# Two token halves of a Strassen feed-forward: chained gate and up products and seven down products in the second half, with operands stored by the first

## The chip, the cores and the metric

The kernel runs on one core of one Trainium2 chip. The metric is the device time of one execution in microseconds, as the median of several runs. All arithmetic is FP32 in the interface; the matrix products are made from FP32R operands that are split into a high part and a low remainder (`ah`/`al`, `wh`/`wl`, `dh`/`dl`), so that one product takes three matmuls per block of the contraction.

## The reference

```
x = A_x                                    # (1, 2048, 576)
sa, ca, ga, sb, cb, gb = split(silu(c) @ w_mod)
h = layernorm(x) * (1 + ca) + sa
x = x + ga * attention(h)                  # 32 heads of 18, 4 segments with a running memory
h = layernorm(x) * (1 + cb) + sb
x = x + gb * ((silu(h @ w_gate) * (h @ w_up)) @ w_down)     # 576 -> 4608 -> 576
```

The change is in the last line, the feed-forward. (One DMA of the attention part moves to another queue.)

## The kernel before, in words

The attention part runs first (up to about 659 us of the profiled execution) and leaves `x` in DRAM as `xD` and its normalized form as `xhD`. The feed-forward then works on the 2048 tokens in two halves (`t` = 0, 1) of 1024 tokens, and in each half on 18 pairs (`p`) of 128-wide blocks of the 4608 hidden columns. A pair is a 2x2x2 problem: two blocks of 512 tokens (`b`), two blocks of 288 inputs, two blocks of 128 hidden columns (`f`).

**Gate and up.** For each pair, gate (`z` = 0) and up (`z` = 1) are each computed with seven products in Winograd's form of Strassen's method instead of eight. Such a product (`m` = 1 to 7, in the order `MO7`) has 7 matmuls of 512 columns into one PSUM bank of tag `M`, of which there are four: three for each of two blocks of 128 inputs, and one that holds the last 32 inputs in three copies, for its high and low parts. So a pair has 14 steps, `k` = 0 to 13, of one product each. VectorE (DVE) adds the products up: each of `m` = 6 and 7 is added to running sums `T[0]`, `T[1]`, `m` = 5 is used twice, and `fin` adds a sum to a bank, then applies SiLU (gate, ScalarE) or multiplies up by gate (DVE). `SLOT` says which of the seven combined weights in the tile `O` a product reads, and `ACT_OP` which of the seven combined activations in `y`.

**Operands.** `load_o` loads four weight blocks of a (pair, z) into `O` (L1052); `sum_o` makes the other combinations on GpSimd (POOL), 4 for each z (L1056). `prep_w` makes `wh` on ScalarE (ACT) seven steps ahead, `wl` on DVE, and the low part of 32 partitions of the third block on POOL (L1061). The operations that subtract are put in the list `later` and issued one step later. `y` holds the activations of one half; those of half 1 are prepared by `prep2` during half 0 and kept in DRAM as `yD`. `load_y` (L1040) reloads `y` in the last pair of half 0: after each up product `m` of that pair has read its combination, that combination is loaded for half 1, in the order `MO7`.

**Down.** The products of a pair's (silu(gate) * up) with `w_down` are issued during the next pair, one `down` (L1141) at each step `k` = 4 to 11: 12 matmuls of 288 columns for 128 tokens into a two-bank PSUM tile of tag `dn` (two of these), which DVE then adds to the accumulator `acc`. `load_d` loads a block of `w_down` and multiplies it by `gb` on POOL; `prep_d` splits it. Per pair that is 8 x 12 = 96 matmuls, from 8 = 2 (f) x 2 (b) x 2 (halves of the 576 outputs) block products.

Every engine runs its own instructions in the order in which the program issues them, and so does the DMA queue of SyncE (SP), which issues nearly all transfers: a transfer that waits for its buffer holds back those behind it.

## Time and profile before

| | us |
|---|---|
| median of 3 runs (1939.92 to 1940.35) | 1940.22 |
| span of the profiled execution | 1946.8 |
| first feed-forward product to first product of half 1 | 659.2 to 1293.0 |
| half 1, to the end of its last product | 1293.0 to 1933.3 |
| start to start of two pairs in half 1 (18 pairs) | 35.28 |
| PE busy, of the span | 1901.2 (98%) |
| DVE / POOL / ACT busy | 1533.1 / 1020.6 / 824.8 |
| mean granted TensorE clock | 0.993 |

The profile is of one execution, and its span is the time from the first to the last instruction of the program. It is 6.6 us (0.3%) longer than the median of the timed runs. Times in views are counted from the start of the span. PE is TensorE's matmuls, PEld its weight loads. The end of a matmul is modelled, and consecutive ones overlap, so what a matmul costs is read from start to start.

### The profile page before, as it was taken

The numbers are of one execution on the slowest core, as the hardware profiler recorded it, in microseconds if no ns is written. First come the engines' busy times: TensorE is split into PE (matmuls) and PEld (weight loads), VectorE is DVE, ScalarE is ACT, GpSimd is POOL, SyncE is SP. The second block draws the span as 40 slices with busy tenths as digits, with TensorE's granted clock in tenths as the row PEclk, the third lists the DMA queues.
The fourth block names the chain that finished last, engine by engine and source line by source line (L and its number), as shares of the span: only waits on it lengthen the run. The fifth ranks groups of instructions, "written<-read, shape, count | busy, mean of one in ns | idle before, by whom it ended". The sixth has DMA issues, their size and how long they took to land.

```text
span 1946.8 us, 31901 instructions
## 1 busy us (share of the span) xinstructions
PE 1901.2 (98%) x11119; PEld 1593.1 (82%) x11119; DVE 1533.1 (79%) x3218; ACT 824.8 (42%) x1652; POOL 1020.6 (52%) x1396
## 2 busy tenths in 40 slices
...
GB/s 207 244 227 233 203 204 140 131 139 150 136 128 125 92 135 101 89 106 80 80 106 83 82 84 78 60 264 146 74 62 45 74 62 59 60 62 74 62 57 50
DMA packets 114354, 223.59 MB, mean 115 GB/s; under 512 B 22992, under 2 KB 40784, under 8 KB 112720
## 3 DMA queue, kind: packets, MB, share of 16 engines
q1 hardware_dynamic: 111936, 215.61, 34.2%
q0 software_dynamic: 576, 5.11, 0.7%
...
## 4 chain that ended last, share of the span: by engine, by line
PE 88%; DVE 4%; DMA 4%; ACT 1%; issue 1%; POOL 1%; SPq 1%; POOLq 0%; ACTq 0%; DVEq 0%
PE M L1090 39%; PE pd L1152 23%; PE pp L93 4%; PE s L576 4%; PE av L596 4%; PE s L174 4%; PE pv L93 3%; PE pw L694 2%; DMA O<-in_wgu_dram 1%; DMA mD<-mr 1%; PE pn L765 1%; PE pm L429 1%; PE px L617 1%; PE pr L346 1%; DVE y L923 1%
## 5 line engine op out<-in xcount | busy, mean ns | idle before, releaser
L1090 PE MATMUL M<-y,wh 128*128 128x512 f32 x2520 | 792.0, 393 | 5.0 <-DVE cu L1106 2.1
L1090 PEld LDWEIGHTS M<-y,wh 128*128 128x128 f32 x2520 | 473.7, 188 | 101.7 <-issue 3.9
L1067 POOL TENSOR_TENSOR wh<-O,wh 32x128 fp32r<-32x128 f32 x504 | 296.6, 593 | 423.0 <-ACT wh L1065 271.3
L1090 PE MATMUL M<-y,wl 128*128 128x512 f32 x1008 | 394.7, 392 | 0.0
L1059 POOL TENSOR_TENSOR O<-O 128x384 f32<-128x384 f32 x288 | 315.4, 1095 | 75.0 <-DMA O<-in_wgu_dram 42.9
L1152 PE MATMUL pd<-dh,ah 128*128 128x288 f32 x1152 | 340.3, 295 | 0.2 <-DVE acc L1155 0.2
L1152 PE MATMUL pd<-dl,ah 128*128 128x288 f32 x1152 | 340.3, 295 | 0.0
L1152 PE MATMUL pd<-dh,al 128*128 128x288 f32 x1152 | 340.1, 295 | 0.0
L1110 ACT CAST ah<-sg 128x512 fp32r<-128x512 f32 x144 | 89.5, 621 | 547.8 <-DVE sg L1107 422.0
L1155 DVE TENSOR_TENSOR acc<-acc,pd 128x576 f32<-128x576 f32 x288 | 216.5, 752 | 111.8 <-PE pd L1152 108.4
L1066 DVE TENSOR_TENSOR wl<-O,wh 128x256 fp32r<-128x256 f32 x504 | 286.2, 568 | 6.0 <-ACT wh L1065 5.2
L179 DVE CUSTOM_DVE_ANT_0 junk<-s,tri 128x256 bf16<-128x256 f32 (+3 forms) x512 | 228.7, 487 | 77.2 <-PE s L174 69.8
L1065 ACT CAST wh<-O 128x384 fp32r<-128x384 f32 x504 | 242.8, 507 | 0.0
L1152 PEld LDWEIGHTS pd<-dl,ah 128*128 128x128 f32 x1152 | 217.4, 189 | 11.8
L1152 PEld LDWEIGHTS pd<-dh,ah 128*128 128x128 f32 x1152 | 216.7, 188 | 11.6 <-DVE acc L1155 0.6
L579 ACT ACTIVATE Pt<-s 128x512 f32<-128x512 f32 (+1 forms) x352 | 186.5, 559 | 88.1 <-PE s L576 72.0
L1152 PEld LDWEIGHTS pd<-dh,al 128*128 128x128 f32 x1152 | 216.6, 188 | 0.0
L1090 PEld LDWEIGHTS M<-y,wl 128*128 128x128 f32 x1008 | 190.0, 188 | 29.6
L1102 ACT ACTIVATE sg<-sg 128x512 f32<-128x512 f32 x144 | 91.2, 633 | 222.7 <-DVE sg L1101 222.7
L576 PE MATMUL s<-qs,ks 110*128 110x512 f32 (+2 forms) x384 | 150.5, 409 | 5.7 <-DMA qs<-mD 4.4
L174 PE MATMUL s<-ks,qs 108*128 108x256 f32 (+3 forms) x512 | 141.2, 327 | 3.3 <-DMA ks<-kD 1.4
L583 POOL TENSOR_SCALAR_AFFINE_SELECT Pt<-Pt 128x512 f32<-128x512 f32 x128 | 81.6, 648 | 100.6 <-ACT Pt L579 100.2
...
## 6 DMA issues: line engine op xcount, KB each, us to landing
...
```

The lines of the kernel that those rows point to most:

```text
L93: nc.tensor.matmul(ps, lhsT=a, rhs=b, start=(k == 0), stop=(k == 13))
L174: nc.tensor.matmul(bank[:, n * (h - h0):n * (h - h0) + n], lhsT=qst[b][0:108, h, 128 * i:128 * i + 128], rhs=kst[b][0:108, h // 2, 0:n], s ...
L179: nc.vector.tensor_tensor_reduce(junk[:, :n], bank[:, n * (h - h0):n * (h - h0) + n], tri[:, L - n:], 1.0, -3e38, op0=ALU.add, op1=ALU.max ...
L576: nc.tensor.matmul(bank[:, n * (g - h):n * (g - h + w)].rearrange("p (a b) -> p a b", a=w), lhsT=kst[u % NB][0:110, g // 2, 128 * j:128 * ...
L579: nc.scalar.activation(pt[:, h:h + per, :n], bank[:, :n * per].rearrange("p (a b) -> p a b", a=per), AF.Exp, scale=SCALE)
L1059: nc.gpsimd.tensor_tensor(o[:, d], o[:, a], o[:, b], op=op)
L1065: nc.scalar.copy(wh, o)
L1066: later.append(lambda: nc.vector.tensor_tensor(wl, o[:, 0:2], f32(wh[:, 0:2]), op=ALU.subtract))
L1067: later.append(lambda: nc.gpsimd.tensor_tensor(wh[32:64, 2], o[32:64, 2], f32(wh[32:64, 2]), op=ALU.subtract))
L1090: nc.tensor.matmul(bank, lhsT=a, rhs=b, start=(n == 0), stop=(n == 6))
L1152: nc.tensor.matmul(pd[:, h, :288], lhsT=a[:, tk], rhs=w[:, f, sl], start=(k == 0), stop=(k == 5))
L1155: nc.vector.tensor_tensor(o, o, pd[:, :, :288], op=ALU.add)
```

## The change

Half 0 keeps its method, its product order (now `MO0`) and its four `M` banks, but stores what it has prepared for use by half 1: the three or four combined weight blocks (`store_o` to `oD`), the split third blocks (`store_r` to `rD`), and the scaled `w_down` blocks (to `wdD`) with the three combinations that POOL now adds (`sum_d`; one more in place). Half 1 loads all these (`load_o`, `prep_r`, `load_d` with `t` = 1) and does none of these sums.

The third blocks of all seven weights of a (pair, z) are split in one go (`prep_r`: one ACT copy of 896 columns and one POOL subtraction on 32 partitions). `prep_w` covers the other two blocks, and runs five steps ahead (`PF`) instead of seven.

In half 1 the sums of products are formed in PSUM where possible. The order of products becomes 1, 5, 6, 2, 7, 4, 3. Bank A gathers products 1, 6, 7, 4; ACT copies product 1 from A to bank B, where product 2 is added to it; bank C gathers 5 and 3. ACT copies A out after products 6 (`tb`) and 7 (`tc`); DVE adds these to C.  There are two A banks and one each of B and C.

The down products of pairs 0 to 15 of half 1 also take seven block products instead of eight: `sum_a` makes four activation combinations on DVE, `prep_a` splits seven operands, and `down` issues chunks of 6 matmuls, 14 chunks per pair = 84 matmuls, at the steps given by `CH`. Each of the seven products has its own accumulator; `comb` adds these up in the last pair. Half 0, and pairs 16 and 17 of half 1, use eight block products (`plain`, 8 chunks of 12). The staging tile `st` of `prep2` has one buffer instead of two. The store of `vs` in the attention part moves from POOL's queue to ACT's.

```diff
@@ -31,7 +31,15 @@
-WR = 10
+WR = 8
+PF = 5
+NSG = 7
+CH = (1, 1, 1, 1, 2, 1, 0, 1, 1, 1, 1, 2, 1, 0)
+CH0 = (0, 1, 1, 0, 1, 1, 0, 1, 0, 1, 1, 1, 0, 0)
+RS = {(0, 5): 2, (0, 6): 4, (0, 8): 3, (0, 10): 5, (1, 9): 2, (1, 11): 3, (1, 13): 4}
+KS = (0, 1, 2, 3)
+KA = ((5, 2), (6, 4), (7, 6), (3, 8))
+ASRC = {5: (1, 1), 6: (0, 0), 7: (0, 1), 3: (1, 0)}
...
-WW = (19, 23, 25, 26, 27, 29, 30)
+WW = (19, 23, 25, 27, 30)
...
+
+    wdD = [dr.tile([P, 7, 288], F32, tag=f"wd{p}", name=f"wd{p}") for p in range(NF // 2)]
+    oD = [[dr.tile([P, 4, 3, P], F32, tag=f"oD{p}_{z}", name=f"oD{p}_{z}") for z in range(2)] for p in range(NF // 2)]
+
+    rD = [[dr.tile([96, 7, P], F32, tag=f"rD{p}_{z}", name=f"rD{p}_{z}") for z in range(2)] for p in range(NF // 2)]
...
-                nc.gpsimd.dma_start(vD[s], vs[s])
+                nc.scalar.dma_start(vD[s], vs[s])
...
-    MO7 = (1, 2, 6, 7, 4, 5, 3)
+    MO0 = (1, 2, 6, 7, 4, 5, 3)
+    MO7 = (1, 5, 6, 2, 7, 4, 3)
...
-            st = x2p.tile([P, 2, 256], F32R, tag="st", name="st", bufs=2)
+            st = x2p.tile([P, 2, 256], F32R, tag="st", name="st")
...
-    def load_o(p, z):
+    def load_o(t, p, z):
         O[p, z] = o = opl.tile([P, 7, 3, P], F32, tag="O", name="O", bufs=2)
-        nc.sync.dma_start(o[:, 0:4], wgu[p, z])
+        if t == 0:
+            nc.sync.dma_start(o[:, 0:4], wgu[p, z])
+        else:
+            nc.sync.dma_start(o[:, 1:4], wgu[p, z][:, 1:4])
+            nc.sync.dma_start(o[:, 0], oD[p][z][:, 0])
+            nc.sync.dma_start(o[:, 4:7], oD[p][z][:, 1:4])
+
+    def store_o(p, z):
+        nc.sync.dma_start(oD[p][z][:, 0], O[p, z][:, 0])
+        nc.sync.dma_start(oD[p][z][:, 1:4], O[p, z][:, 4:7])
+
+    def prep_r(t, p, z):
+        R[z] = r = wrp.tile([P, 7, P], F32R, tag="wr", name="wr")
+        if t == 1:
+            nc.sync.dma_start(f32(r[0:96]), rD[p][z])
+            return
+        o = O[p, z]
+        nc.scalar.copy(r[0:96], o[0:96, :, 2, :])
+        later.append(lambda: nc.gpsimd.tensor_tensor(r[32:64], o[32:64, :, 2, :], f32(r[32:64]), op=ALU.subtract))
...
+    def store_r(p, z):
+        nc.sync.dma_start(rD[p][z], f32(R[z][0:96]))
+
     def prep_w(p, z, m):
-        o = O[p, z][:, SLOT[m]]
-        wh = wp.tile([P, 3, P], F32R, tag="wh", name="wh")
+        o = O[p, z][:, SLOT[m], 0:2]
+        wh = wp.tile([P, 2, P], F32R, tag="wh", name="wh")
         wl = wp.tile([P, 2, P], F32R, tag="wl", name="wl")
         nc.scalar.copy(wh, o)
-        later.append(lambda: nc.vector.tensor_tensor(wl, o[:, 0:2], f32(wh[:, 0:2]), op=ALU.subtract))
-        later.append(lambda: nc.gpsimd.tensor_tensor(wh[32:64, 2], o[32:64, 2], f32(wh[32:64, 2]), op=ALU.subtract))
+        later.append(lambda: nc.vector.tensor_tensor(wl, o, f32(wh), op=ALU.subtract))
         W[z, m] = (wh, wl)
...
+    def load_d(t, p):
+        RW[p] = r = rp.tile([P, 7, 288], F32, tag="d", name="dr_")
+        if t == 0:
+            for f in range(2):
+                nc.sync.dma_start(r[:, 2 * f:2 * f + 2].rearrange("p a b -> p (a b)"), wd[2 * p + f])
+        else:
+            nc.sync.dma_start(r[:, :NS[p]], wdD[p][:, :NS[p]])
+
+    def mul_d(p, f):
+        v = RW[p][:, 2 * f:2 * f + 2].rearrange("p a b -> p (a b)")
+        nc.gpsimd.tensor_tensor(v, v, gbB, op=ALU.mult)
+
+    def sum_d(p, j):
+        r = RW[p]
+        d, a, b = ((4, 1, 0), (5, 3, 4), (6, 2, 5), (1, 3, 1))[j]
+        nc.gpsimd.tensor_tensor(r[:, d], r[:, a], r[:, b], op=ALU.subtract)
+
+    def prep_d(p, key, slot):
+        r = RW[p][:, slot]
+        dh = dp.tile([P, 288], F32R, tag="dh", name="dh")
+        dl = dp.tile([P, 288], F32R, tag="dl", name="dl")
+        nc.scalar.copy(dh, r)
+        later.append(lambda: nc.vector.tensor_tensor(dl, r, f32(dh), op=ALU.subtract))
+        DP[p % 2, key] = (dh, dl)
+
+    def prod(z, m, bank, first, last):
...
-        ops.append((wh[0:96, 2], y[0:96, o, 4]))
+        ops.append((R[z][0:96, SLOT[m]], y[0:96, o, 4]))
         for n, (a, b) in enumerate(ops):
-            nc.tensor.matmul(bank, lhsT=a, rhs=b, start=(n == 0), stop=(n == 6))
-        return bank
-
-    T, SG, AC = {}, {}, {}
+            nc.tensor.matmul(bank, lhsT=a, rhs=b, start=(first and n == 0), stop=(n == 6),
+                             skip_group_check=not first)
+
...
-    def fin(z, ij, bank, add):
+    def fin(z, ij, bank, add=None):
         if z == 0:
-            SG[ij] = g = tmp("sg", 5)
-            nc.vector.tensor_tensor(g, bank, add, op=ALU.add)
-            nc.scalar.activation(g, g, AF.Silu)
+            SG[ij] = g = tmp("sg", NSG)
+            if add is None:
+                nc.scalar.activation(g, bank, AF.Silu)
+            else:
+                nc.vector.tensor_tensor(g, bank, add, op=ALU.add)
+                nc.scalar.activation(g, g, AF.Silu)
             return
         g = SG.pop(ij)
-        u = tmp("cu", 2)
-        nc.vector.tensor_tensor(u, bank, add, op=ALU.add)
-        (nc.gpsimd if ij in PM else nc.vector).tensor_tensor(g, u, g, op=ALU.mult)
-        ah = ap_.tile([P, L], F32R, tag="ah", name="ah")
-        al = ap_.tile([P, L], F32R, tag="al", name="al")
-        nc.scalar.copy(ah, g)
-        later.append(lambda: nc.vector.tensor_tensor(al, g, f32(ah), op=ALU.subtract))
-        AC[ij] = (ah, al)
-
-    def step(z, m):
-        bank = prod(z, m)
+        if add is None:
+            nc.vector.tensor_tensor(g, bank, g, op=ALU.mult)
+        else:
+            u = tmp("cu", 2)
+            nc.vector.tensor_tensor(u, bank, add, op=ALU.add)
+            nc.vector.tensor_tensor(g, u, g, op=ALU.mult)
+        AC[ij] = g
...
+    def step(z, m):
+        if m == 1:
+            B["A"] = ps.tile([P, L], F32, tag="A", name="A", bufs=2)
+            B["B"] = ps.tile([P, L], F32, tag="B", name="B", bufs=1)
+        elif m == 5:
+            B["C"] = ps.tile([P, L], F32, tag="C", name="C", bufs=1)
+        bank = B["B" if m == 2 else "C" if m in (5, 3) else "A"]
+        prime = "set" not in B
+        prod(z, m, bank, m in (1, 5) or m == 2 and prime, m in (2, 4, 3))
+        if m == 1:
+            if prime:
+                copy_t("cu", bank)
+            else:
+                nc.scalar.copy(B["B"], bank)
+        elif m == 2:
+            fin(z, (0, 0), bank, T["cu"] if prime else None)
+            B["set"] = True
+        elif m == 6:
+            copy_t("tb", bank)
+        elif m == 7:
+            copy_t("tc", bank)
+            fin(z, (1, 1), B["C"], T["tc"])
+        elif m == 4:
+            fin(z, (1, 0), bank)
+        elif m == 3:
+            fin(z, (0, 1), bank, T["tb"])
+
+    def prep_a(par, m, src):
+        ah = ap_.tile([P, L], F32R, tag="ah", name="ah")
+        al = ap_.tile([P, L], F32R, tag="al", name="al")
+        nc.scalar.copy(ah, src)
+        later.append(lambda: nc.vector.tensor_tensor(al, src, f32(ah), op=ALU.subtract))
+        AP[par, m] = (ah, al)
+
+    def sum_a(j):
+        d, a, b, op = (((1, 1), (0, 1), (1, 1), ALU.add), ((0, 1), (0, 0), (0, 1), ALU.subtract),
+                       ((0, 0), (1, 1), (0, 0), ALU.subtract), ((1, 0), (1, 0), (0, 0), ALU.subtract))[j]
+        nc.vector.tensor_tensor(PA[d], PA[a], PA[b], op=op)
...
+    def down(t, p, c):
+        m, c = POS[c // 2], c % 2
+        ah, al = AP[p % 2, m]
+        dh, dl = DP[p % 2, m]
+        pd = psd.tile([P, 2, L], F32, tag="dn", name="pd", bufs=2)
+        for i in range(2):
+            tk = slice(128 * (2 * c + i), 128 * (2 * c + i) + 128)
+            for k, (a, w) in enumerate(((ah, dh), (ah, dl), (al, dh))):
+                nc.tensor.matmul(pd[:, i, :288], lhsT=a[:, tk], rhs=w, start=(k == 0), stop=(k == 2))
+        o = acc[m][:, 2 * c:2 * c + 2]
+        if p == 0 and m not in (2, 3, 4):
+            nc.vector.tensor_copy(o, pd[:, :, :288])
+        else:
+            nc.vector.tensor_tensor(o, o, pd[:, :, :288], op=ALU.add)
...
+    def plain(t, p, c):
+        b, h, c = c // 4, c // 2 % 2, c % 2
+        pd = psd.tile([P, 2, L], F32, tag="dn", name="pd", bufs=2)
+        for i in range(2):
...
-                ah, al = AC[f, b]
+                ah, al = AP[p % 2, (f, b)]
+                dh, dl = DP[p % 2, (f, h)]
                 for a, w in ((ah, dh), (ah, dl), (al, dh)):
-                    nc.tensor.matmul(pd[:, h, :288], lhsT=a[:, tk], rhs=w[:, f, sl], start=(k == 0), stop=(k == 5))
+                    nc.tensor.matmul(pd[:, i, :288], lhsT=a[:, tk], rhs=w, start=(k == 0), stop=(k == 5))
                     k += 1
...
+        if p == NPR - 1 and (t or c == 1):
+            store(t, b, h, d, c if t else None)
+
+    def comb(j):
+        d, b = ((2, 1), (0, 5), (6, 1), (5, 6), (3, 5), (7, 6), (4, 7), (0, 7))[j]
+        d = acc[d] if d else x11[1]
+        nc.vector.tensor_tensor(d, d, acc[b], op=ALU.add)
...
+        seq = [(t, p, z, m) for t in range(2) for p in range(NPR) for z in range(2) for m in (MO7 if t else MO0)]
...
+        for p in range(NPR):
+            nx = (p + 1) % NPR
+            tn = 0 if nx else 1
+            par[0] = p % 2
+            if p == NPR - 1:
+                run(g2)
+            for k in range(14):
+                z, m = k // 7, MO0[k % 7]
+                todo, later[:] = later[:], []
+                prep_w(*seq[n + PF][1:])
...
+                step0(z, m)
+                if p == NPR - 1 and z:
+                    load_y(ACT_OP[m])
+                if k == 7 - PF:
+                    load_o(tn, nx, 0)
+                elif k == 14 - PF:
+                    load_o(tn, nx, 1)
+                if tn == 0 and 4 <= k < 8:
+                    sum_o(nx, 0, k - 4)
+                elif tn == 0 and k >= 11:
...
+                if k == 0 and p == 0:
+                    store_o(p, 0)
+                elif k == 9 and tn == 0:
+                    store_o(nx, 0)
+                elif k == 3:
+                    store_r(p, 0)
+                    store_o(p, 1)
+                elif k == 6:
+                    store_r(p, 1)
+                if k == 2:
+                    prep_r(0, p, 1)
+                elif k == 9:
+                    prep_r(tn, nx, 0)
+                if prev is not None and DS <= k < DS + 8:
+                    plain(*prev, k - DS)
+                if k == 1:
+                    load_d(0, p)
+                elif k in (5, 6):
+                    mul_d(p, k - 5)
+                elif 8 <= k < 12 and p < NPR - 2:
+                    sum_d(p, k - 8)
+                elif k == 13:
+                    nc.sync.dma_start(wdD[p][:, :NS[p]], RW[p][:, :NS[p]])
...
+                if k in G2 and p > 0:
+                    next(g2, None)
+            prev = (0, p)
+        p6.close()
+        accq = pool(p4, "acq")
+        new_acc(accq, (1, 6, 7))
+        ps = pool(p4, "ps4", 1, space=PSUM)
+        for p in range(NPR):
...
+            chunk = 0
+            for k in range(14):
...
+                step(z, m)
+                if not last and k == 7 - PF:
+                    load_o(1, nx, 0)
+                if not last and k == 14 - PF:
+                    load_o(1, nx, 1)
+                if k == 2:
+                    prep_r(1, p, 1)
+                if not last and k == 9:
+                    prep_r(1, nx, 0)
+                if is_plain(*prev):
+                    if k == 0 and prev[0]:
+                        prep_a(prev[1] % 2, (0, 1), PA[0, 1])
+                    if CH0[k]:
+                        plain(*prev, chunk)
+                        chunk += 1
+                else:
+                    for j in range(4):
+                        if k == KS[j]:
+                            sum_a(j)
+                    for j, kk in KA:
+                        if k == kk:
+                            prep_a(prev[1] % 2, j, PA[ASRC[j]])
+                    for _ in range(CH[k]):
+                        down(*prev, chunk)
+                        chunk += 1
...
+                if k == 2:
+                    load_d(1, p)
+                if is_plain(1, p):
+                    if k in (4, 5, 6, 7):
+                        prep_d(p, ((k - 4) // 2, k % 2), k - 4)
+                elif k >= 7:
+                    prep_d(p, POS[k - 7], WSLOT[POS[k - 7]])
+                for ij, kk, j in (((0, 0), 11, 1), ((1, 1), 12, 4), ((1, 0), 13, 2)):
+                    if k == kk:
+                        prep_a(p % 2, ij if is_plain(1, p) else j, AC[ij])
...
+        flush()
+        prep_a(prev[1] % 2, (0, 1), PA[0, 1])
+        for c in range(8):
+            plain(*prev, c)
+            if c == 0:
                 flush()
```

178 lines of the change are left out of this document (89 added, 89 removed).

## The prediction

> **What bounds the kernel now.** I read the page first, then the chain of waits over the feed-forward, then busy times by window, and last the engines' timelines at the two places that the change touches most.
>
> The page and the chain:
>
> ```profile
> PE 1901.2 (98%) x11119; PEld 1593.1 (82%) x11119; DVE 1533.1 (79%) x3218; ACT 824.8 (42%) x1652; POOL 1020.6 (52%) x1396
> ...
> 1856.30 11.28 PE M L1090 x49
> 1891.58 11.28 PE M L1090 x49
> 1928.47 3.19 PE pd L1152 x24
> 1933.26 9.57 PE pd L1152 x72
> ```
>
> The chain in half 1 is PE alone. Its columns are start, duration, what, count: 49 gate/up matmuls of 512 columns take 11.28, so one is 0.230 us; 72 down matmuls of 288 columns take 9.57, so one is 0.133. A pair is 98 x 0.230 + 96 x 0.133 = 35.3, and the starts above lie 35.28 apart: PE issues without a gap. So time goes only with matmuls, or comes back as a PE wait.
>
> Windows (length, busy us of PE, PEld, DVE, ACT, POOL, granted clock, DMA share, GB/s):
>
> ```profile
> 1330.20:1894.60 564.40, 564.40 (x3105) 499.66 (x3104) 460.43 (x739) 207.21 (x416) 321.41 (x387) 1.00 0.20 67
> 1295.00:1300.00 5.00, 4.91 (x22) 3.75 (x21) 4.55 (x9) 2.84 (x6) 1.41 (x3) 1.00 1.01 347
> 1300.00:1305.00 5.00, 4.73 (x26) 3.96 (x25) 3.14 (x6) 1.98 (x5) 0.70 (x1) 1.00 1.01 347
> 650.00:652.70 2.70, 0.40 (x2) 0.06 (x2) 2.64 (x4) 2.70 (x8) 2.54 (x3) 0.50 0.42 109
> 652.70:658.50 5.80, 5.78 (x24) 5.80 (x25) 5.64 (x7) 1.29 (x4) 5.56 (x8) 0.50 0.13 51
> 658.50:660.00 1.50, 1.50 (x10) 1.37 (x9) 1.47 (x4) 0.00 (x0) 1.42 (x3) 0.96 0.00 0
> ```
>
> Row 1: half 1 is PE-bound with DVE second, busy 82%. Rows 2 and 3: where the halves meet, the DMA engines are full, at 347 GB/s. Rows 4 to 6, before the feed-forward: PE idles, the granted clock is 0.50, and it stays there for 5.8 us of unbroken matmuls.
>
> Timelines: SP issuing `y`, PE meeting it, one PE wait on ACT, and DVE back to back:
>
> ```profile
> 1275.37 0.33 SPq L1041 DMA_DIRECT2D y<-yD  x1
> 1291.37 0.32 SPq L1041 DMA_DIRECT2D y<-yD  x1
> 1303.44 0.47 PE L1090 MATMUL M<-y,wh 128*128 128x512 f32 x1 [0.27 <-DMA y<-yD]
> 1264.09 0.50 PE L1090 MATMUL M<-y,wh 128*128 128x512 f32 x1 [0.25 <-ACT tx L1118]
> 1408.80 0.42 DVE L1066 TENSOR_TENSOR wl<-O,wh 128x256 fp32r<-128x256 f32 x1
> 1409.13 0.69 DVE L1101 TENSOR_TENSOR sg<-M,ty 128x512 f32<-128x512 f32 x1
> 1410.58 0.76 DVE L1155 TENSOR_TENSOR acc<-acc,pd 128x576 f32<-128x576 f32 x1 [0.77 <-PE pd L1152]
> 1411.25 0.42 DVE L1066 TENSOR_TENSOR wl<-O,wh 128x256 fp32r<-128x256 f32 x1
> ```
>
> Lines 2 and 3: the load of the sixth combination of `y` (product 5) is issued at 1291.4 and lands at about 1303.2: it queues behind five others. Line 4: a matmul whose wait came late starts 0.5 after its turn, though PE idles only 0.25. DVE start to start: 0.33 for 256 columns, 0.67 for 576; 512 columns take 0.60 back to back and 0.72 with the next one depending on it (both from the same timeline).
>
> **Part by part, against the profiled span of 1946.8.** It is 6.6 us above the median; I carry the difference in us over to the median.
>
> *Seven down products (a gain).* Pairs 0 to 15 of half 1 issue 84 down matmuls instead of 96. 12 x 0.133 = 1.6 us of PE per pair, all on the path: 16 x 1.6 = **-25.5**. Everything else is what gives this back.
>
> *The order 1, 5, 6, ... and the reload of `y`.* Half 1's second product is now 5, but its combination of `y` can be reloaded only after half 0's last product 5, which is sixth. Today 1.245 MB per combination is queued; product 5's is needed sixth, at 1303.1, and PE loses 1.9 us in that pair (start to start 37.14 against 35.28). After: the first half 1 product starts at 1293.0, product 5 is due at 1294.6. Ahead of its data in SP's queue, from 1275.4 on: six combinations (7.47 MB), and the load of `O` for up at step 9, now seven blocks (1.38 MB instead of 0.79) plus `rD` (0.34). That is 9.2 MB; at 347 GB/s 26.5 us, and some 2.4 for start and completion (the same sum for today's queue, held until 1280.4 by `O`'s buffer, needs that to meet 1303.2): 1304.3. PE waits 9.7; less today's 1.9: **+8**. From below, an empty queue would still give 1291.4 + 1.245/0.347 + 2.4 = 1297.4, so +1; from above, a busier queue +9.5.
>
> *The clock after that wait.* PE idles longer than in rows 4 to 6, so I expect the 0.50 state again. By rows 5 and 6, 5.8 us at half rate, half of it lost: **+2.9**. The lower bound is 0, if the clock stays as it does through the three short waits at 1300 to 1307. The Trainium skill ("TensorE: Matmul & The Clock Gate", section "What's actually happening") says that the full clock returns after about 3.4 us of sustained work; by that the loss is 1.7, an estimate, and the sum 1.2 lower; rows 5 and 6 show longer than that.
>
> *Chained banks and DVE in half 1.* DVE loses work (`T` additions; POOL, idle now, no longer slows it: `wl` has minimum 406, median 421, maximum 1653 ns), and gains `sum_a` (4), three more `al`, and 14 additions of 576 instead of 8. Per pair: 14 `wl` x 0.33, 19 operations of 512 x 0.60 (8 adds and multiplies, 7 `al`, 4 `sum_a`), 7 `dl` of 288 x 0.37 (between the rows of 256 and 512), 14 `acc` x 0.67 = 28.0 of 33.7 us. Enough, but uneven. Walk from the end of product 7 of `up` (step 11): ACT's copy `tc` ends 0.84 later (0.2 after the last start, 0.58 its own time). DVE then has, in order: add, multiply, two `acc`; `wl`, `dl`, `al`, multiply, `acc`; `wl`, `dl`, `al`; and the add that frees bank C: 0.60 + 0.72 + 1.34 + 0.33 + 0.37 + 0.60 + 0.60 + 0.67 + 0.33 + 0.37 + 0.60 + 0.69 = 7.2, so C is free at 8.1. PE needs C for the next pair's product 5 after four chunks and three products, 4 x 0.80 + 3 x 1.61 = 8.03. About 0.1 late, plus 0.2 to 0.3 that a late wait costs beyond its idle time (line 4 above): 0.4 per pair, **+6.4** for 16. Bounds: 0, if DVE is a tenth of a us earlier; 1.0 per pair (16 us) if each of these twelve operations takes 0.05 more. The other new waits have cover: A after product 7 has two chunks (1.6) against 0.84 for ACT's copy; B's copy has 3.2; the two `dn` tiles are each free by the next use, since at step 12 the `acc` ends at 3.0 and PE comes at 3.2. If ACT were late there by 0.6, each pair would pay about 0.5 twice.
>
> *The loads of half 1.* 4.5 MB per pair, 133 GB/s on average. The tightest: at step 2 `O`, `rD` and `wdD` (2.75 MB, 8 us at 347 GB/s, some 10.5 with issue and completion) against 12 us until `prep_d` at step 7. Hidden; without that cover ACT would stop at `prep_d`, and PE 8 us later.
>
> *Half 0.* PE's work is unchanged. POOL: 7 or so us of small subtractions become two of 32x896 (a 128-column one takes 0.45, a 384-column sum 1.02, so about 2.2 each) and four sums of 288: even. SP issues about 5 more transfers per pair at 0.4, each able to wait: `load_d` now waits for the store of `wdD` to land, and holds `load_o` behind it by some 4 us; POOL's sums behind `load_o` catch up by step 8, and `prep_w` needs them at step 11. ACT stands behind POOL at `prep_r` (steps 2 and 9) with 3 us to spare. The one-buffer `st` makes ACT wait for a transfer every second step; the cover is four `M` banks, but there ACT's copy `tx` ends only 0.6 to 1.8 us before PE needs its bank at step 4. I take **+1**: up to +6 if each of 17 pairs stalls 0.35; down to -2, since two of seven `wl` (0.4 to 1.6 each) leave the stretch before the first product, where DVE is full. The first pair moves about 8.6 MB in 23 us, at the limit of 347 GB/s, but only stores queue late: nothing.
>
> *Tail.* The last pair now leaves all eight chunks behind its last product; the first needs `al` of (1,0), queued on DVE behind that product's add and multiply: 0.2 + 0.69 + 0.72 + 0.60 = 2.2 against 0.67 of matmuls before it. **+1.8** (1.4 to 2.2). `comb` adds 8 x 1.3 of DVE (estimated on from 512 and 576 columns) where it has 5 us to spare in 35: nothing. Moving the store of `vs`: POOL spent 0.6 four times, off the path: nothing.
>
> Sum: -25.5 + 8 + 2.9 + 6.4 + 1 + 1.8 = **-5.4**: span 1941.4, median **1934.8**.
>
> **Rivals.**
>
> *DVE becomes the bound of half 1 (slower).* The walk above ends 0.1 from the edge with twelve operations in it. If each carries 0.08 more (a semaphore instruction on DVE is 0.02 to 0.05, a dependency 0.11), C is 1.1 late and a pair pays 1.4: 16 x 1.4 = 22.4 instead of 6.4, median 1951. It turns to slower by over 0.2% from 0.98 us per pair on (-25.5 + 13.7 + 16 x 0.98 = 3.9). For it: single banks B and C, and DVE busiest just there. Against: POOL idle, and 82% busy today without one PE wait. Chance 0.25.
>
> *No stall in half 1's pairs.* If the walk ends 0.1 earlier: 1934.8 - 6.4 = 1928.4 (1925 if the clock holds). Chance 0.24.
>
> *The stores disturb half 0.* If `tx`'s slack goes in every pair, 17 x 0.5 = 8.5 instead of 1: 1942.3. For it: slack of 0.6 in some pairs; against: the waits sit mostly at other steps. Chance 0.15, no change.
>
> That the change does not do what it says would be PE idling out the 1.6 us in every pair; that is the first rival at its full price.
>
> **How the numbers follow.** A measurement of this kernel can tell 0.2%, 3.9 us, from no change. The forecast case, 0.36, spans about 1931 to 1939, 0.28 of it faster and 0.08 no change. Faster 0.28 + 0.24 = 0.52; same 0.08 + 0.15 = 0.23; slower 0.25. The low ends together, with the `y` wait at 6, give -25.5 + 6 + 0 + 0 - 2 + 1.4 = -20.1, so 1920 is the low end; the high end reaches into the DVE rival, 1948. The forecast's own range is 1928 to 1940.
>
> **What would show it.** Right: half 1 pairs of 33.7 to 34.2 start to start, a PE wait near 1294 of 8 to 10 us on `y`, a granted clock of 0.50 for some us behind it, PE waits on DVE at product 5, POOL near idle in half 1. Wrong: pairs above 34.8 (DVE bound), half 0 pairs above 36, or a `y` wait under 4.

## The result

The kernel after takes 1986.94 us (median of four runs, 1984.65 to 1994.11) against 1940.28 in the same comparison: a ratio of 1.0242, 95% interval 1.0222 to 1.0261. It is slower by 46.7 us, where 1934.8 (5.4 us faster) was forecast. The profiled execution has a span of 1982.9 us.

Five stretches of the two profiled executions say where the time lies:

| us | before | after | difference | forecast |
|---|---|---|---|---|
| start to the first feed-forward product | 659.2 | 656.4 | -2.8 | 0 |
| half 0 | 633.9 | 677.8 | **+43.9** | +1 |
| first pair of half 1 | 37.1 | 49.4 | +12.3 | +10.9 |
| the next 16 pairs of half 1 | 564.4 | 544.9 | -19.5 | -19.1 |
| start of the last pair to the end | 52.1 | 54.4 | +2.3 | +1.8 |

The differences add up to 36.2 us, the difference of the two spans; the medians lie 46.7 apart, and no stretch of the profiles shows the rest.

One row is wrong, and it is most of the error. (About 1.2 of the 43.9 us are the first product of half 0, which runs at a granted clock of 0.50 after the change and at full clock before it.)

First the busy line of the kernel after's page, then windows of it (length; busy us of PE, PEld, DVE, ACT, POOL; granted clock; DMA share; GB/s). The windows are half 0, the 16 steady pairs, and five pieces of the first pair of half 1.

```profile
PE 1893.7 (96%) x10927; PEld 1564.1 (79%) x10927; DVE 1596.6 (81%) x3375; ACT 889.1 (45%) x1928; POOL 649.0 (33%) x808
```

```profile
656.40:1334.20 677.80, 644.93 (x3446) 553.75 (x3445) 620.40 (x919) 261.09 (x590) 362.04 (x300) 0.99 0.54 177
1383.60:1928.50 544.90, 544.90 (x2913) 474.45 (x2913) 463.11 (x864) 260.57 (x606) 0.00 (x0) 1.00 0.41 135
1337.00:1344.50 7.50, 0.50 (x1) 0.19 (x1) 2.25 (x5) 2.02 (x5) 0.00 (x0) 0.59 1.04 329
1344.50:1348.00 3.50, 0.00 (x0) 0.01 (x1) 0.00 (x0) 0.00 (x0) 0.00 (x0) 0.50 0.99 308
1348.00:1350.50 2.50, 2.48 (x6) 2.02 (x7) 0.00 (x0) 0.00 (x0) 0.00 (x0) 0.50 0.88 315
1351.50:1352.00 0.50, 0.50 (x4) 0.50 (x3) 0.00 (x0) 0.00 (x0) 0.00 (x0) 0.53 0.18 74
1352.00:1353.00 1.00, 1.00 (x10) 1.00 (x9) 0.00 (x0) 0.00 (x0) 0.00 (x0) 1.00 0.05 18
```

The same window of half 0 in the kernel before:

```profile
659.20:1293.00 633.80, 629.45 (x3445) 553.77 (x3445) 557.83 (x889) 253.60 (x519) 381.07 (x462) 1.00 0.29 97
```

In half 0 PE loads the same number of weights (x3445) and idles 33 us instead of 4. POOL, as forecast, has no more to do (362 us for 381). DVE, with 30 more instructions, is busy 62.6 us longer. In the steady pairs of half 1 PE is busy throughout and POOL does nothing.

The first pair of half 1, as PE's timeline. In square brackets: idle time before the row, and what ended it:

```profile
1335.37 0.39 PE L1136 MATMUL A<-y,wh 128*128 128x512 f32 x1
1337.11 0.50 PE L1136 MATMUL A<-y,wr 96*128 96x512 f32 x1 [1.35 <-DMA wr<-rD]
1348.03 0.76 PE L1136 MATMUL C<-y,wh 128*128 128x512 f32 x1 [10.42 <-DMA y<-yD]
```

That is the forecast wait on `y` for product 5, and behind it the clock of 0.50 (windows above).

What stops PE in half 0, as the sum of its waits over half 0 (line, waited for, us in total, times, longest), before and then after:

```profile
PE M L1090 <- DVE cu L1106: 2.1, 2, 1.5
```

```profile
PE M L1136 <- DVE cu L1158: 23.9, 22, 3.8
PE M L1136 <- ACT tb L1180: 7.2, 13, 2.5
```

PE waits for a bank that DVE has not read yet. The wait for ACT's copy `tb` has DVE behind it too: in 12 of the 13 cases ACT came to the copy late because its `ah` just before had waited 1.5 to 2.6 us for DVE's `sg`, as here (the thirteenth, 2.5 us in the last pair, follows a wait for the transfer out of `st`):

```profile
956.84 0.62 ACT L1226 CAST ah<-sg 128x512 fp32r<-128x512 f32 x1 [1.84 <-DVE sg L1159]
```

DVE's groups in half 0 (line, operation, tiles, count, busy us, mean ns of one), before and after:

```profile
L1066 DVE TENSOR_TENSOR wl<-O,wh 128x256 fp32r<-128x256 f32 x254 | 147.7, 582 | 2.9 <-ACT wh L1065 2.2
L1107 DVE TENSOR_TENSOR sg<-cu,sg 128x512 f32<-128x512 f32 x71 | 53.4, 752 | 2.4
L1125 DVE TENSOR_TENSOR ty<-M,tx 128x512 f32<-128x512 f32 x36 | 24.6, 684 | 2.7 <-PE M L1090 2.5
```

```profile
L1101 DVE TENSOR_TENSOR wl<-O,wh 128x256 fp32r<-128x256 f32 x252 | 190.5, 756 | 4.1 <-ACT wh L1100 0.5
L1159 DVE TENSOR_TENSOR sg<-cu,sg 128x512 f32<-128x512 f32 x70 | 59.6, 852 | 2.4
L1187 DVE TENSOR_TENSOR tc<-M,tb 128x512 f32<-128x512 f32 x36 | 24.5, 681 | 0.8 <-PE M L1136 0.6
```

The same operation on the same shape takes longer: `wl` 756 ns instead of 582, and `sg` (a multiplication of two SBUF tiles) 852 instead of 752. An addition that reads a PSUM bank has not changed (681 for 684). One case in the timelines of DVE and POOL:

```profile
1211.90 3.76 DVE L1101 TENSOR_TENSOR wl<-O,wh 128x256 fp32r<-128x256 f32 x1
```

```profile
1211.55 0.91 POOL L1051 TENSOR_TENSOR ha<-ha 96x256 f32<-96x256 f32 x1
1212.43 2.96 POOL L1091 TENSOR_TENSOR O<-O 128x384 f32<-128x384 f32 x3
```

This `wl` normally lasts 0.42. It ends at 1215.66, 0.28 after the last of four POOL operations that follow each other without a gap. Of the 252 `wl` in half 0 after, 63 last over 1 us, against 27 of 254 before; every one of these 90 ends 0.28 or 0.29 after a POOL operation ends. The Trainium skill ("SBUF — State Buffer", section "Who interferes with whom") says that a VectorE instruction with two SBUF inputs contends with a GpSimd instruction that reads SBUF, that the second to start waits for the first, and that one SBUF input doesn't contend. The rows agree on which operations stretch, `wl` and `sg` but not `tc`. They differ on the order: three of the four GpSimd operations above start after this `wl`, and it still ends behind them.

The steps of a pair show where it matters. A step with a down product takes 3.24 us, one without (12, 13 and 0 to 3) 1.62, and DVE has its product's work in both. In the mean over pairs 2 to 17 of half 0, steps 0 to 3 go from 1.61, 1.62, 1.62, 1.64 to 1.78, 2.23, 2.44, 2.26; the others hardly change.

### The profile page after: what moved, and what is told of

It is laid out like the page before. It is cut to its first block, busy times and chain, and to the rows that moved or that the text cites. A ratio compares the mean times of both kernels' runs of the same rounds, so it can differ in the third digit from the quotient of the medians.

```text
span 1982.9 us, 31199 instructions
## 1 busy us (share of the span) xinstructions
PE 1893.7 (96%) x10927; PEld 1564.1 (79%) x10927; DVE 1596.6 (81%) x3375; ACT 889.1 (45%) x1928; POOL 649.0 (33%) x808
## 4 chain that ended last, share of the span: by engine, by line
PE 71%; DVE 17%; DMA 5%; issue 3%; ACT 3%; POOL 1%; SPq 0%; ACTq 0%; DVEq 0%; POOLq 0%
PE A L1136 12%; PE pd L1266 9%; PE M L1136 8%; PE pd L1283 8%; PE C L1136 6%; PE s L589 4%; PE av L609 4%; PE pp L101 4%; PE s L187 4%; PE B L1136 3%; DVE wl L1101 3%; PE pv L101 2%; PE pw L707 2%; DVE dl L1126 2%; DVE sg L1159 2%
## 5 line engine op out<-in xcount | busy, mean ns | idle before, releaser
L1136 PE MATMUL M<-y,wh 128*128 128x512 f32 x1008 | 362.6, 400 | 32.6 <-DVE cu L1158 23.9
L1136 PEld LDWEIGHTS M<-y,wh 128*128 128x128 f32 x1008 | 191.3, 190 | 85.9 <-issue 31.7
L1136 PE MATMUL A<-y,wh 128*128 128x512 f32 x576 | 202.7, 392 | 0.0
L1136 PE MATMUL M<-y,wl 128*128 128x512 f32 x504 | 199.6, 396 | 0.0
L1100 ACT CAST wh<-O 128x256 fp32r<-128x256 f32 x504 | 198.3, 401 | 0.0
L1283 PE MATMUL pd<-dl,ah 128*128 128x288 f32 x640 | 188.9, 295 | 0.0
L1091 POOL TENSOR_TENSOR O<-O 128x384 f32<-128x384 f32 x144 | 161.9, 1132 | 76.0 <-DMA oD<-O 18.5
L1271 DVE TENSOR_TENSOR acc<-acc,pd 128x576 f32<-128x576 f32 x216 | 159.0, 748 | 23.5 <-PE pd L1266 21.9
L1287 DVE TENSOR_TENSOR acc<-acc,pd 128x576 f32<-128x576 f32 x156 | 116.2, 745 | 57.6 <-PE pd L1283 57.1
L1227 DVE TENSOR_TENSOR al<-sg,ah 128x512 fp32r<-128x512 f32 x192 | 141.8, 738 | 24.3 <-ACT ah L1226 24.0
L1086 POOL TENSOR_TENSOR wr<-O,wr 32x896 fp32r<-32x896 f32 x36 | 77.1, 2142 | 202.4 <-ACT wr L1085 187.8
```

Of the source, the lines that this page charges most:

```text
L1091: nc.gpsimd.tensor_tensor(o[:, d], o[:, a], o[:, b], op=op)
L1100: nc.scalar.copy(wh, o)
L1136: nc.tensor.matmul(bank, lhsT=a, rhs=b, start=(first and n == 0), stop=(n == 6), skip_group_check=not first)
L1227: later.append(lambda: nc.vector.tensor_tensor(al, src, f32(ah), op=ALU.subtract))
L1271: nc.vector.tensor_tensor(o, o, pd[:, :, :288], op=ALU.add)
L1283: nc.tensor.matmul(pd[:, i, :288], lhsT=a[:, tk], rhs=w, start=(k == 0), stop=(k == 5))
```

## The experiments

The changes are made in the kernel after, unless it says otherwise. The kernel before took 1940 to 1946 us in the different comparisons, so kernels are compared by their ratio to it, and parts by the profile. "Pairs" is the sum of pairs 2 to 17 of half 0 (the first two vary with the end of the attention part); DVE and POOL are busy us in half 0; "first" and "steady" are pair 0 and the mean of pairs 1 to 16 of half 1.

| run | ratio [95% interval] | half 0 | pairs | DVE | POOL | first | steady |
|---|---|---|---|---|---|---|---|
| before | 1 | 633.9 | 570.6 | 558 | 381 | 37.1 | 35.28 |
| after | 1.0242 [1.0222, 1.0261] | 677.8 | 610.1 | 620 | 362 | 49.4 | 34.06 |
| e2_nosumd | 1.0139 [1.0101, 1.0176] | 663.2 | 597.4 | 596 | 302 | 48.2 | 34.06 |
| e7_nostore | 1.0185 [1.0155, 1.0214] | 669.8 | 602.8 | 615 | 358 | 47.1 | 34.18 |
| e3_st2 | 1.0218 [1.0188, 1.0248] | 675.8 | 608.1 | 622 | 362 | 49.2 | 34.06 |
| e1_spread | 1.0219 [1.0189, 1.0249] | 684.6 | 615.9 | 589 | 431 | 47.8 | 34.15 |
| e9_dlearly | 1.0223 [1.0202, 1.0243] | 681.4 | 612.9 | 631 | 367 | 48.1 | 34.05 |
| e10_poollight | 1.0082 [1.0061, 1.0102] | 654.7 | 590.5 | 554 | 227 | 48.7 | 34.06 |
| e15_light_st2 | 1.0088 [1.0068, 1.0108] | 651.9 | 588.8 | 552 | 227 | 48.6 | 34.05 |
| e11_nodl | 1.0122 [1.0102, 1.0142] | 661.7 | 597.7 | 583 | 362 | 47.2 | 34.06 |
| e8_chain | 1.0406 [1.0389, 1.0424] | 725.0 | 653.9 | 515 | 356 | 36.9 | 34.07 |
| e4_order | 1.0181 [1.0159, 1.0204] | 680.5 | 612.5 | 622 | 361 | 43.0 | 34.07 |
| e12_pieces | 1.0245 [1.0225, 1.0266] | 684.4 | 613.7 | 600 | 432 | 45.0 | 34.57 |
| e13_half1 | 1.0142 [1.0123, 1.0161] | 662.3 | 593.5 | 582 | 373 | 44.5 | 34.56 |
| e19_before5 | 1.0021 [1.0010, 1.0033] | 641.1 | 578.6 | 590 | 390 | 35.3 | 35.29 |
| e16_lead7 | 1.0137 [1.0113, 1.0162] | 662.0 | 594.8 | 611 | 359 | 48.7 | 34.13 |
| e17_l7half1 | 1.0033 [1.0021, 1.0045] | 643.9 | 574.9 | 557 | 360 | 43.0 | 34.56 |
| e18_l7h1dl | 1.0037 [1.0026, 1.0049] | 644.8 | 573.2 | 554 | 360 | 42.6 | 34.57 |
| e20_back | 0.9997 [0.9987, 1.0007] | 640.5 | 573.5 | 547 | 347 | 43.4 | 34.14 |
| e21_back2 | 0.9984 [0.9975, 0.9994] | 637.0 | 573.5 | 556 | 354 | 44.7 | 34.22 |

Where an edit leaves half 0 alone (e4), its pairs came out 2.4 above the kernel after; differences of up to 3 are taken as nothing.

### GpSimd's work, or the stores

**e2_nosumd** drops the four sums of the down weights; uncombined blocks are stored in their place:

```diff
-                elif 8 <= k < 12 and p < NPR - 2:
-                    sum_d(p, k - 8)
```

> The four POOL sums of w_down blocks per pair are left out of half 0; half 1 gets uncombined blocks in their place, so its values are not the reference's, and all its transfers and matmuls are kept. Theory P: 22 us of stretch of DVE go, and half 0 takes 655 to 668. Theory S: half 0 stays at 674 to 681.

**e7_nostore** stores only pair 0's operands, which half 1 then loads for every pair:

```diff
-                elif k == 9 and tn == 0:
-                    store_o(nx, 0)
-                elif k == 3:
+                elif k == 3 and p == 0:
                     store_r(p, 0)
                     store_o(p, 1)
-                elif k == 6:
+                elif k == 6 and p == 0:
...
-                elif k == 13:
+                elif k == 13 and p == 0:
```

> Half 0 stores its prepared operands for pair 0 only, and half 1 loads those of pair 0 for every pair (its values are not the reference's; all its transfers, sums and matmuls are kept). Theory P: half 0 takes 670 to 680, since POOL does the same. Theory S: with some 5 transfers less per pair on SP, half 0 takes 636 to 650.

**e3_st2** gives `st` its second buffer back:

```diff
-            st = x2p.tile([P, 2, 256], F32R, tag="st", name="st")
+            st = x2p.tile([P, 2, 256], F32R, tag="st", name="st", bufs=2)
```

> The staging tile of the preparation of half 1 has two buffers again. ACT waited 32 us in half 0 for the transfer out of the one buffer. Theory P: those waits were ACT's to spare; half 0 takes 672 to 680. Theory S: ACT's lateness reaches PE, and half 0 loses 15 to 30 us: 648 to 663.

**e1_spread** splits the third blocks in one piece per product, and copies `wr` ahead of `wh`:

```diff
-        later.append(lambda: nc.gpsimd.tensor_tensor(r[32:64], o[32:64, :, 2, :], f32(r[32:64]), op=ALU.subtract))
...
+        if t == 0:
+            s, o3, r = SLOT[m], O[p, z], R[z]
+            later.append(lambda: nc.gpsimd.tensor_tensor(r[32:64, s], o3[32:64, s, 2, :], f32(r[32:64, s]), op=ALU.subtract))
```

> Half 0 (first feed-forward product to first product of half 1) took 677.8 us after the change and 633.8 before. Here the low part of the third weight block is again subtracted in pieces of 128 columns on POOL, one piece per step, instead of 896 columns at once. Theory P (long or unbroken POOL work holds up DVE operations on two SBUF operands, and DVE comes late to the turn of the pair): the 47 us by which DVE operations are stretched beside the 896-column piece fall to about 13, as before; half 0 takes 645 to 658. Theory S (the new stores and loads hold up SP and ACT): half 0 stays at 674 to 681.

Without the sums the pairs lose 12.7 us, without the stores 7.3, and the second `st` buffer changes nothing. So of these three GpSimd's work weighs most, and the stores something. e1 is a miss: DVE is busy 31 us less, yet the pairs are 5.8 us longer. The short steps, further down, show why.

### Which part of VectorE's and GpSimd's work

**e9_dlearly** moves the splits of the down weights out of the turn:

```diff
-                if 8 <= k < 12:
-                    prep_d(p, ((k - 8) // 2, k % 2), k - 8)
+                if k in (6, 7):
+                    for s in (2 * (k - 6), 2 * (k - 6) + 1):
+                        prep_d(p, (s // 2, s % 2), s)
```

> In the first half the four splits of the down weights (ScalarE's copy dh, VectorE's difference dl) are issued two each at steps 6 and 7, instead of one each at steps 8 to 11; all else as in the kernel after. Theory D (VectorE is too full at the turn of the pair): four dl of 0.6 us leave the turn, at most 2.4 us a pair of the 2.7 lost; part of that comes back where steps 6 to 9 get fuller, so the first half falls by 10 to 25 us, to 653 to 668, total 1962 to 1977. Rival S (the work that GpSimd and the queues got, not the place of the differences): no change within 5 us, 1982 to 1992.

**e10_poollight** has e2's edit, and drops GpSimd's 32-row subtraction too:

```diff
-        later.append(lambda: nc.gpsimd.tensor_tensor(r[32:64], o[32:64, :, 2, :], f32(r[32:64]), op=ALU.subtract))
```

> In the first half GpSimd's four sums of the down weights a pair and its 32-row subtraction a reload are left out (what is stored and used in their place isn't the sum, so the computation is incomplete; the stores keep their sizes). All else as in the kernel after. Theory D, with GpSimd's part of it (VectorE's operations with two SBUF operands last longer while GpSimd works, in all 143.9 us of such lengthening in the first half after against 69.8 before): the lengthening falls to 65 to 85 us and the first half to 635 to 655 us, total 1945 to 1965. If the place of dl alone is the cause: the lengthening falls as well, but the first half stays above 665.

**e15_light_st2** is e10 with e3's edit.

> As the run without GpSimd's sums of the down weights and its 32-row subtraction (which are left out again), and st has two buffers. That run's first half was 654.7 us although VectorE had as much to do as in the kernel before (554 us against 558.5), 21 us over the kernel before; ScalarE there waited 45.2 us for the store of the one st, and TensorE 6 to 12 us for ScalarE's copy tb. If that is what is left: the first half falls to 638 to 646 us. Rival (with st the wait only moves; the rest is the order of VectorE's work, or the stores): 650 to 656.

**e11_nodl** drops DVE's `dl` in half 0 (`half[0]` is 0 there), where the products use `dh` in its place:

```diff
-        later.append(lambda: nc.vector.tensor_tensor(dl, r, f32(dh), op=ALU.subtract))
+        if half[0]:
+            later.append(lambda: nc.vector.tensor_tensor(dl, r, f32(dh), op=ALU.subtract))
+        else:
+            dl = dh
```

> In the first half VectorE's four differences dl of a pair are left out (the plain down products take dh in their place, so their small parts are wrong there); GpSimd's work, ScalarE's copies, the stores and the products stay as in the kernel after. Theory V (the first half is held up by VectorE's total: 34 to 38 us of work in pairs of 36 to 43, wherever in the pair it is put, which is why moving dl alone brought nothing): VectorE's work falls by 45 to 50 us, and by what the runs without sums gave (24 us less gave 14.6, 66 less gave 23) the first half falls by 15 to 28 us, to 650 to 663, the total to 1960 to 1974. Rival W (GpSimd's own pace: its results come late, VectorE's lengthening is only seen beside them): GpSimd does the same work, the first half stays at 673 to 680.

**e8_chain** uses the chained `step` in half 0 too:

```diff
-    MO0 = (1, 2, 6, 7, 4, 5, 3)
+    MO0 = (1, 5, 6, 2, 7, 4, 3)
...
-                step0(z, m)
+                step(z, m)
```

> The first token half also uses the chained step (products in the order 1, 5, 6, 2, 7, 4, 3, the sums of products made in PSUM); the prepared operands are summed and stored as in the kernel after. Theory D (the first half is bound at the turn of each pair by how much VectorE has to do in steps 9 to 13 and 0 to 3, which the moved differences of the down weights and the moved GpSimd work have filled): the chained step takes four sums of M-products a half pair from VectorE, about 8 x 0.6 us a pair, which is more than it is late by, so the first half falls from 677.8 to 625 to 645 us although GpSimd's work stays. As y is then reloaded in the order of the second half, the junction pair goes from 49.4 to 37 to 41 us. Together 1925 to 1945 us. Rival S (the stores, SyncE's queue or ScalarE's copies themselves hold the pair up, VectorE is only seen beside them): ScalarE gets more copies, the first half stays at 665 to 685 us, only the junction moves, 1965 to 1980 us.

Four results. The place of `dl` is not the cause (e9). DVE is on the path: with GpSimd's work as it is, 37 us less for DVE shorten the pairs by 12.4 (e11), so GpSimd's own pace is not all. With less work on GpSimd (227 us, less even than before the change, since the split of the third blocks is missing too) DVE is at 554 us, for 558 in the kernel before, and the pairs lose 19.6 (e10); yet 20 us remain, and they are not `st` (e15). And DVE's total is not the measure: e8 has the least of all runs and the longest half 0, 725 us where 625 to 645 was expected. PE's waits in half 0 of e8:

```profile
PE C L1136 <- DVE cu L1158: 44.7, 24, 3.6
```

There is one bank C where there were four M banks, and PE stands when DVE reads it late. The theory in the form "VectorE's total, wherever it is put" falls here. What is left is narrower: PE stops when DVE is late at a bank, and DVE is late in the short steps when GpSimd holds it up there.

### The first pair of half 1

**e4_order** takes product 5 sixth in that pair:

```diff
+    MOJ = (1, 6, 2, 7, 4, 5, 3)
...
-                z, m = k // 7, MO7[k % 7]
+                z, m = k // 7, (MO7 if p else MOJ)[k % 7]
```

> Only the first pair of the second half is changed: its products go in the order 1, 6, 2, 7, 4, 5, 3, so that the operand y of product 5, which comes as the last of the reloads that the first half's last pair leaves, is wanted sixth and not second. Theory: the junction pair's extra 12 us against a steady pair are the wait for that operand and the lower clock after it; the pair falls from 49.4 to 37 to 41 us, the total by 9 to 12 us, to 1975 to 1978; the first half stays at 678 within 2. Rival (the junction waits on the chain of pair 0's own operands, or on VectorE's backlog): the pair stays above 45.

The pair falls from 49.4 to 43.0, half of what there was to gain and short of the 37 to 41 expected. What is late next is another wait, in PE's and ACT's timelines:

```profile
1341.12 0.50 PE L1137 MATMUL A<-y,wr 96*128 96x512 f32 x1
1344.98 0.50 PE L1137 MATMUL A<-y,wh 128*128 128x512 f32 x1 [3.36 <-ACT cu L1165]
```

```profile
1343.52 0.62 ACT L1230 CAST ah<-sg 128x512 fp32r<-128x512 f32 x1 [1.83 <-DVE sg L1160]
1344.05 0.40 ACT L1101 CAST wh<-O 128x256 fp32r<-128x256 f32 x1
1344.35 0.58 ACT L1165 COPY cu<-A 128x512 f32<-128x512 f32 x1
```

Product 6 may go into bank A only when ACT has copied product 1 out of it. ACT stands in order behind two `ah` of half 0's last pair, which wait 3.0 and 1.8 us for DVE's `sg`: the late DVE of half 0 reaches over into half 1. In e8, whose half 0 uses half 1's order and so reloads `y` in it, the pair takes 36.9.

### Short pieces, and the sums in the second half

**e12_pieces** splits the third block as the kernel before does, in both halves; `wr`, its store and its load go:

```diff
+        later.append(lambda: nc.gpsimd.tensor_tensor(wh[32:64, 2], o[32:64, 2], f32(wh[32:64, 2]), op=ALU.subtract))
...
-        ops.append((R[z][0:96, SLOT[m]], y[0:96, o, 4]))
+        ops.append((wh[0:96, 2], y[0:96, o, 4]))
```

> The third block of each operand is split as in the kernel before, in both halves: wh is three blocks wide, GpSimd subtracts 32 x 128 elements right behind each wh, the tile wr with its 32 x 896 subtraction, its store and its load go. All else as in the kernel after. Theory V: the 32 x 896 subtraction lengthens VectorE's work by 47.4 us in the first half, fourteen short ones a pair did it by 12.6 in the kernel before; so VectorE has 30 to 40 us less, and without the two stores a pair the first half falls by 15 to 28 us, to 650 to 663. In the second half GpSimd's 14 short pieces a pair cost VectorE some 0.7 us of the 5 that it has over: steady pairs stay at 34.05 to 34.3. Total 1960 to 1975. Rival (short pieces do the same harm, since they lie in the 1.6 us steps too, as in the run that spread them): the first half stays above 673.

**e13_half1** is e12 with e3's and e4's edits, and the sums of the down weights in half 1:

```diff
                 if k == 2:
                     load_d(1, p)
+                elif 5 <= k < 9 and not is_plain(1, p):
+                    sum_d(p, k - 5)
```

> As the run with short pieces, and besides: the four sums of the down weights go to the second half (steps 5 to 8 of its pairs, from four stored parts), st has two buffers, and the first pair of the second half takes product 5 sixth. Theory V: the first half has only the work of the kernel before and the stores of the O sums and of four down parts: 638 to 650 us; junction pair 41 to 45; in the second half the sums lengthen VectorE's work by 1.2 us a pair and the pieces by 0.7, with 29 of 34 us busy so far: steady pairs 34.1 to 34.7. Total 1932 to 1950, about the kernel before or up to 0.5% under it. Rival (VectorE becomes the bound of the second half as it did in the first): steady pairs 35.2 us or more, total above 1950.

e12 is a miss like e1: over the half short pieces hold DVE less, and they help nothing here. GpSimd then has 432 us of work, and three times in the first two pairs PE waits for GpSimd itself, which it never does in the kernel after:

```profile
PE M L1137 <- POOL wh L1102: 5.0, 3, 2.8
```

e13 takes the sums away as well, and the pairs lose 20.2 against e12. Half 0 stays 28 us above the kernel before, at 662.3, where 638 to 650 was expected. Half 1's pairs take 34.56 instead of 34.06, with the pieces in both runs.

What e1 and e12 missed shows when busy time is taken over the short steps alone (the six from step 12 of one pair to step 3 of the next; us, in the mean over pairs 2 to 17):

| run | length | DVE busy | POOL busy |
|---|---|---|---|
| before | 9.77 | 8.95 | 3.49 |
| after | 12.00 | 11.19 | 4.14 |
| e1_spread | 12.38 | 11.68 | 8.23 |
| e12_pieces | 12.14 | 11.34 | 7.42 |
| e13_half1 | 11.00 | 10.39 | 5.88 |
| e11_nodl | 10.83 | 10.00 | 3.94 |
| e10_poollight | 10.81 | 9.98 | 2.95 |
| e7_nostore | 11.39 | 10.57 | 3.03 |

In all runs of this document but e8 the stretch is 0.6 to 0.9 us longer than DVE's busy time in it: its length goes with DVE's busy time there, and the kernel before had only these 0.8 us to spare. In e1 and e12 DVE's busy time falls in the other eight steps (21.6 and 22.5 us, for 23.9 in the kernel after), and GpSimd's pieces lie beside the short ones.

### The lead

One part of the change was left: operands five steps ahead instead of seven, hence loads of `O` two steps later, with GpSimd's sums of `O` behind them.

**e19_before5** puts only that into the kernel *before*:

```diff
-WR = 10
+WR = 8
...
-                    if z == 0:
-                        prep_w(p, 1, m)
-                    elif not last:
-                        prep_w(nx, 0, m)
+                    if n + 5 < len(seq):
+                        prep_w(*seq[n + 5])
+                    n += 1
...
-                    if not last and k % 7 in (3, 4, 5, 6):
-                        sum_o(nx, k // 7, k % 7 - 3)
+                    if not last and 4 <= k < 8:
+                        sum_o(nx, 0, k - 4)
+                    elif not last and k >= 11:
+                        sum_o(nx, 1, k - 11)
```

> The kernel before with one thing changed: each operand pair wh, wl is made five steps ahead of its product and not seven (eight buffers, not ten), so each load of O is issued two steps later (steps 2 and 9) and GpSimd's sums of O follow at steps 4 to 7, 11 to 13 and 0. Theory L (the shorter lead, which the change brought with it, puts the load's landing and GpSimd's sums of O beside the 1.6 us steps 12, 13 and 0 to 3, where VectorE has no slack): pairs of the first half go from 35.7 us to 36.3 to 37.2, the first half from 634 to 645 to 660 us, the second half's pairs from 35.3 to 35.3 to 36.3; total 1952 to 1985. Rival N (the lead costs nothing; what remains over the kernel before in the runs with little GpSimd work is the smaller and later dl and the stores): first half 632 to 638, total within 5 us of the kernel before.

**e16_lead7** gives half 0 of the kernel after its lead of seven back:

```diff
-                prep_w(*seq[n + PF][1:])
+                prep_w(*seq[n + 7][1:])
...
-                if k == 7 - PF:
+                if k == 0:
                     load_o(tn, nx, 0)
-                elif k == 14 - PF:
+                elif k == 7:
                     load_o(tn, nx, 1)
...
+                if tn == 0 and k % 7 in (3, 4, 5, 6):
+                    sum_o(nx, k // 7, k % 7 - 3)
```

> The kernel after with the lead of the kernel before in the first half: operands seven steps ahead (ten buffers there, two of them given back at the half), loads of O at steps 0 and 7, GpSimd's sums of O at steps 3 to 6 and 10 to 13; the second half keeps five steps. Everything else of the change stays. Theory L: the first half falls from 677.8 by the 15 to 25 us that remained when GpSimd's added work was gone, to 650 to 663, total 1960 to 1973. Rival N: 672 to 682, total 1980 to 1990.

The lead counts in both. In the kernel before it costs 8.0 us of the pairs, and a ratio of 1.0021 (half 1, without the staging for the next half, pays nothing); half 0 takes 641.1, less than the 645 to 660 expected. In the kernel after, taking it back saves 15.3. Of the short steps GpSimd's sums of `O` fill 1.1 us a pair in the kernel before, 3.3 in e19 and in the kernel after, and 1.9 in e16. In e19 DVE has the work of the kernel before and is busy 32 us longer with it, `sg` above all (994 ns in the mean for 752), and PE's new wait in pairs 2 to 17 is for ACT's copy `tx`, six times of seven behind an `ah` that waited for DVE's `sg`:

```profile
L1107 DVE TENSOR_TENSOR sg<-cu,sg 128x512 f32<-128x512 f32 x71 | 70.6, 994 | 2.4
```

```profile
PE M L1090 <- ACT tx L1118: 5.8, 7, 1.3
```

In e16 `sg` is back from 852 to 759 ns. So the lead reaches PE, at least in part, as GpSimd's other work does: through the operations of DVE beside it.

### Both together

**e17_l7half1** is e13 with e16's edit.

> The run with short pieces and the sums of the down weights in the second half, with the lead of seven in the first half besides. Theory L with V: nothing of the first half is left that the kernel before doesn't have but the stores and the place of dl, so it falls from 662.3 to 638 to 648 us; junction pair 42 to 46 and steady pairs 34.5 to 34.7 as in that run; total 1941 to 1953, level with the kernel before or up to 0.5% over. Rival N: 658 to 664, total 1963 to 1973.

**e18_l7h1dl** is e17 with e9's edit.

> As the run before it, and the four dl of a pair at steps 6 and 7 instead of 8 to 11, about where the kernel before had its two. If the late dl still holds the turn up once GpSimd's work is back where it was: the first half another 3 to 10 us shorter, 632 to 642, total 1935 to 1947. If its place costs nothing, as it did in the kernel after: within 2 us of the run before it.

With both taken back the pairs are at 574.9 and 573.2, for 570.6 before: 37 of the 39.5 us are accounted for, near the sum of the two alone (19.6 from e10, which leaves out more, and 15.3 from e16). The short steps are back at 9.79 us in e18, with DVE busy 8.99. The two runs agree within the interval: the place of `dl` costs nothing once more. The stores of `O` and of the `w_down` blocks are still there (e20 below has those of the third blocks too, at 573.5), so by themselves the stores cost little. Half 0 of e18 as a whole is still 11 us above the kernel before; 8.4 of them lie in its first two pairs, where PE waits 4.2 us for an operation of the attention part and the granted clock is 0.50 for 6.8 us, and the half starts 5.1 us earlier. Half 0 of e18 as a window, and PE's wait for DVE's `cu` in it:

```profile
654.10:1298.90 644.80, 635.13 (x3446) 556.00 (x3446) 554.31 (x925) 258.73 (x555) 359.72 (x456) 0.99 0.48 157
```

```profile
PE M L1140 <- DVE cu L1162: 4.2, 3, 1.6
```

### Does the change keep a gain?

**e20_back** is e18, but with the pieces written into `wr`, which is stored and loaded, so that half 1 has none:

```diff
+        if t == 0:
+            if m == 1:
+                R[z] = wrp.tile([P, 7, P], F32R, tag="wr", name="wr")
+            s, o3, r = SLOT[m], O[p, z], R[z]
+            nc.scalar.copy(r[0:96, s], o3[0:96, s, 2, :])
+            later.append(lambda: nc.gpsimd.tensor_tensor(r[32:64, s], o3[32:64, s, 2, :], f32(r[32:64, s]), op=ALU.subtract))
```

> Built from the kernel after with what the runs so far point to: the lead of seven in the first half, the sums of the down weights in the second half (steps 5 to 8), the dl of the first half at steps 6 and 7, two buffers for st, product 5 sixth in the second half's first pair. The third blocks are split in short pieces as in the kernel before, but into the tile wr, which is stored, so that the second half loads it and GpSimd has no pieces there. Theory L with V: first half 640 to 648 us as in the run before this with pieces; steady pairs of the second half 34.05 to 34.2, since the 34.59 came with the pieces; junction pair 42 to 45. Total 1936 to 1946, 0.1 to 0.5% under the kernel before. If the 34.59 came from the four sums or the wider copies: steady pairs stay at 34.5 or more, total 1944 to 1952.

**e21_back2** also makes the `O` sums of half 1's pairs 0 and 1 again instead of storing and loading them:

```diff
-        if t == 0:
+        if t == 0 or p < 2:
             nc.sync.dma_start(o[:, 0:4], wgu[p, z])
```

> As the run before it, and the O tiles of the second half's first two pairs are not stored and loaded whole: four of seven parts are loaded as in the first half, and GpSimd, idle there, makes the sums again. That takes 2.4 MB from the transfers around the junction, where the DMA engines were busy 1.03 of the time and the products wait for y. If the junction pair is bound by these transfers: 42.6 falls to 38 to 41 us, total 2 to 5 us under the run before it. If it is bound by the order in which y comes: within 1 us of it.

e20 is level with the kernel before (0.9997, interval 0.9987 to 1.0007): its steady pairs are back at 34.1, so the 34.6 came with GpSimd's pieces in half 1. e21 is faster by 0.16%, with an interval of 0.06 to 0.25%. The reason given for it failed: with 2.4 MB less to move the first pair took 44.7, not 38 to 41. PE waits in it 2.4 us for ACT's copy as in e4 (below), has a granted clock of 0.50 for 3.4 us behind that, and waits 3.0 us for DVE at bank C near the pair's end. Why the median is 3 us lower than e20's is not shown. PE's timeline of e21:

```profile
1302.20 0.50 PE L1145 MATMUL A<-y,wh 128*128 128x512 f32 x1 [2.36 <-ACT cu L1173]
```

In e20's profile most of the gain of the steady pairs (about 18 us) is used up by the first pair (+6.3), half 0 (+6.6) and the tail (+2.3).

## Why the prediction was wrong

*Seven down products and DVE in half 1: right.* Forecast -25.5 and +6.4, measured -19.5 together. A pair takes 34.06, where PE's own work would be 33.7 and 34.1 was forecast. The lateness lies where the walk had put it, at bank C of product 5, which starts a row late behind a chunk:

```profile
1453.89 0.29 PE L1266 MATMUL pd<-dh,al 128*128 128x288 f32 x1
1454.08 0.50 PE L1136 MATMUL C<-y,wh 128*128 128x512 f32 x1
1454.42 0.40 PE L1136 MATMUL C<-y,wl 128*128 128x512 f32 x1
```

(0.19 and 0.34 from start to start, for 0.13 and 0.23.) The DVE rival, at 1.4 a pair of half 1, did not happen: DVE became the bound in half 0.

*The reload of `y`: right in mechanism, sized too small.* Product 5 starts at 1348.03, 13.8 after the half's first product and 12.2 late, for 9.7 forecast. The wait on `y` itself is 10.4 us. The part left out is a wait of 1.35 on `wr<-rD`, in the product before.

*The clock behind it: right in mechanism, sized too large.* It stayed at 0.50 from 1348.03 to about 1352.0, 3.9 us, so 1.9 are lost and not 2.9. The Trainium skill's 3.4 us of sustained work ("TensorE: Matmul & The Clock Gate", section "What's actually happening") is nearer. The 5.8 us from ahead of the feed-forward were no measure, because the granted clock changes on a grid of 3.41 us in these traces: it is low from 648.39 to 658.63 before (3 x 3.41) and from 1338.32 to 1351.97 after (4 x 3.41). PE's unbroken work began at 652.7 and at 1348.03, 2.5 and 0.5 us ahead of a point of the grid, and both times the clock came back one point later, at the end of the first 3.41 us in which PE was busy throughout.

The two errors have opposite signs, 2.3 too little for the wait and 1.0 too much for the clock, so that 12.3 for 10.9 is in part luck.

*Tail:* +2.3 for +1.8.

*Half 0: the step that failed.* The prediction ended its count of POOL's work with "even", and took +1, at most +6; it was +43.9, and its own sign of being wrong, half 0 pairs above 36, came: 38.1 in the mean. The sum over POOL was right (362 for 381 us) and was the wrong question. POOL's time counted as off the path, but a POOL operation also stops a DVE operation beside it, and that costs PE time in the short steps, where DVE was busy 8.95 of 9.77 us before the change already. The prediction had the clue in hand, `wl` with a minimum of 406 and a maximum of 1653 ns ("POOL, idle now, no longer slows it"), and used it for half 1 alone: DVE was walked through there, and never in half 0, although it was busy 88% of it (557.83 of 633.8). The runs put the sums of the down weights at 12.7 us of the pairs (e2; 20.2 between e12 and e13). The second half of the miss is an edit that got no price for the pairs: the lead went from seven steps to five with the loads and sums of `O` behind it, 15.3 us (e16). With both taken back 36.9 of the 39.5 us are gone (e18).

*The rivals.* "The stores disturb half 0" had the right half and, in the main, the wrong cause: leaving the stores out takes 7.3 us of 39.5 (e7), and with the other causes gone they cost under 3 (e20). None had GpSimd in it.

*From span to median.* 6.6 us were carried over as the distance of the profiled run from the median; in the kernel after the span lies 4.0 below its median. That is 10.6 of the 52 us between forecast and result, and no run shows where it comes from.

What stays open: how much of the shorter lead's cost comes through the place of the sums of `O`, which the longer `sg` of e19 points to, and how much because fewer operands lie ready when DVE is late (no run separates the two); why e7 gains 7.3 us without the stores (its short steps hold 3.0 us of GpSimd's work instead of 4.1); and which of DVE's operations in the turn is the decisive one.
